# Linear attention and a Sinkhorn-routed MoE on one core: q transposed as loaded, phi read from PSUM, two scalings on GpSimd, two more units in seven products, and a new front order

## The chip, the cores and the metric

The kernel runs on one core of a Trainium2 chip. The metric is the device time of one execution in microseconds (us), lower being better: the median of the runs shown. A core has five instruction streams that matter here: TensorE (PE) multiplies matrices, VectorE (DVE) and ScalarE (ACT) work elementwise and read and write both SBUF and PSUM, GpSimd (POOL) works elementwise and issues most loads, and SyncE (SP) issues the other DMAs. Each runs its instructions in order and waits at semaphores for the others.

## The reference

Attention with B = 8, H = 8, S = 576, d = 64, then a mixture of experts on x, the attention's result as 4608 x 512:

```python
phi = lambda x: np.where(x > 0, x, np.exp(x) - 1.0) + 1.0
kv  = np.einsum('bhsd,bhse->bhde', phi(k), v)
z   = phi(k).sum(2)
x   = (phi(q) @ kv) / (phi(q) @ z[..., None] + 1e-6)   # then (B*S, H*d) = (4608, 512)
P   = np.exp(x @ w_gate - max)
for _ in range(8):
    P /= P.sum(1, keepdims=True) + 1e-9
    P /= P.sum(0, keepdims=True) + 1e-9
    P *= N / E                                      # 4608 / 8
out = sum(P[:, e:e+1] * (np.maximum(x @ w1[e], 0) @ w2[e]) for e in range(8))   # F = 1024
```

## The kernel before, in words

All matrices are multiplied in fp16. phi(x) is computed as min(max(x + 1, 1), exp(x)). x is kept transposed in SBUF, as xT (128 x 4 x 4608).

**The front: 16 head pairs.** A call of `att(b, g)` (L385) handles four heads of one batch, n = 2b + g. Its steps: load k, q, v (L406); exp(k) on ACT (L417), max(k + 1, 1) and min on DVE (L421, L425); kv and z by 36 small matmuls with tiles of 64x64 (L446), copied to kvz (L359 on ACT or L361 on DVE). For q: exp on ACT (L477), max(q + 1, 1) on DVE into tq (L480), min on DVE (L484), 36 transposes on PE from tq into the PSUM bank pair att (L469), and a copy out of PSUM to qpT (L361, L359). Then the denominator (four matmuls of 288 columns, L504), its logarithm on ACT (L516, one for each half c of the tokens), one exp of minus the logarithm for both halves (L521), the numerator (L504), and the product of both, which writes half a row pair of xT (L531). k and q of n = 0 come as f32 on SP's queue; the other q and v come as fp16 over GpSimd's queue, which converts, with k in f32 there too. Buffers for k, q and v are three deep, and a load that reuses one waits on GpSimd for the users of its buffer; everything behind it on that queue waits with it.

**The MoE.** Tokens come in nine blocks g of 512. For expert 0 layer 1 is plain (`layer1`, hq at L717: per block 8 tiles of 4 matmuls with 512 columns; relu on ACT or DVE, L722 and L724). The first block's first four tiles are computed in two halves: first the two c rows that head pair 0 gives, then those of head pair 1. Layer 2 of expert 0 is plain in some blocks (`unit_plain`, L1017: 32 matmuls of 512 columns, four copies out of PSUM) and in the others a block product in seven instead of eight parts (`unit` and `layer2`, L1133: 56 matmuls of 256 columns, four sums S of hb on DVE at L1104, and evictions in halves at L1146 to L1151). Which blocks do which is set by the constants NS = 6, NL = 4, NG = 9 in the loop at L1255 to L1265. Experts 1 to 7 run in products throughout, from about 190 us on, with their sums of weights W and T (L1059, L1073), sums S (L1104), layer-1 products (L832), and weighted evictions on DVE (L1164) and on ACT and GpSimd (L1171, L1174). SP stores x in blocks to DRAM for them (L745, L747, L780).

**The Sinkhorn** (L560 to L606) keeps the exponentials P_sb (128 x 36 x 8) and finds row and column factors Rr and cc. In each of eight iterations f_a, on DVE, does: wt = P0 * cc (L577, not in the first), sum over experts (L574 or L579), factor (L580, L581), wt = P0 * Rr written transposed (L582), and sum over tokens (L584). PE sums over partitions with a matrix of ones (L589), and f_d on DVE gives cc (L593 to L598). At the end P = P0 * cc * Rr (L604, L605). It runs from about 125 to 176 us, between the layer-1 and layer-2 units of expert 0.

**What sets the order.** Nothing is issued as the code stands. `_Plan` (L18) collects tasks with their engines, costs, dependencies and buffer slots. Its `run` places them one by one: those of the string `_FRONT` (L141) first, in exactly that order (task number and engine letter), and the rest by earliest time and priority. So each engine's instruction order is written out by hand for the front and expert 0, and follows the costs given to `add` behind that.

**The beginning.** GpSimd's load queue starts k1, v0, k2, q1, v1, q2, v2, w1 (its first 512 columns), q3, k3, w1 (the rest), v3, q4, w2 in two pieces. w1 and w2 belong to expert 0. Until data are there PE runs dummy matmuls on a zeroed tile (`f_warm`, L621, tile yw), 46 in all.

## Time and profile before

| | |
|---|---|
| median of 3 runs | 952.09 us (951.47 to 952.39) |
| the profiled execution | 951.94 us |
| its span, first to last instruction | 950.1 us |
| mean granted TensorE clock | 0.999 |
| DVE, ACT, POOL busy | 765.3, 575.8, 144.3 us |

How to read it: the span is cut into stretches, and for each the busy time of each engine is given. An instruction's row has its start, its length, engine, line, operation, output and input tiles, and in brackets the idle time of the engine just before it with what ended that. A group's row has the count, the total, the mean in ns, and the idle time before the group's members. Matmuls are pipelined: the modelled end of one lies behind the start of the next, so the distance between starts is the cost.

### The profile page before, as it was taken

Reading aid. Unit: us, or ns where it says so; the run is one execution under the profiler, and the core shown is the slowest. Engines: PE = TensorE matmul, PEld = TensorE weight load, DVE = VectorE, ACT = ScalarE, POOL = GpSimd, SP = SyncE. Lnnn points to the kernel's source line nnn. Section 1 sums busy time; section 2 is a strip of 40 time slices with the busy share of each in tenths; the row PEclk is TensorE's granted clock in tenths of the full one; section 3 lists DMA queues with packets and bytes.
Section 4 is the critical chain, followed back from the end, with each engine's and each line's share of the span. In section 5 each row is a group of like instructions: output and inputs, shape, how many; then the busy total and the mean of one; then the engine's idle time right before and its main releaser. Section 6 shows DMA issues by size and latency. Waiting matters only on the chain.

```text
span 950.1 us, 19908 instructions
## 1 busy us (share of the span) xinstructions
PE 939.9 (99%) x7816; PEld 631.7 (66%) x7816; DVE 765.3 (81%) x1479; ACT 575.8 (61%) x1025; POOL 144.3 (15%) x204
## 2 busy tenths in 40 slices
PE   9999999999999999999999999999999999999997
PEld 4444478666676666766677666766667666776665
DVE  7699899879877888788887888878887888877776
ACT  6899856666655555555555555555555555555552
POOL 5433100011111111110011111111112111111110
PEclk9999999999999999999999999999999999999999
DMA  9989793452254222652236222652226422215544
GB/s 239 265 185 235 170 230 94 122 122 78 79 126 86 75 77 78 162 122 78 79 87 119 79 78 78 152 114 70 68 67 143 111 78 78 73 45 166 167 134 134
DMA packets 82042, 112.75 MB, mean 119 GB/s; under 512 B 7324, under 2 KB 46236, under 8 KB 81948
## 3 DMA queue, kind: packets, MB, share of 16 engines
q1 hardware_dynamic: 56876, 75.59, 26.0%
q0 software_dynamic: 24320, 34.78, 19.6%
q8 instruction: 61, 1.00, 0.4%
q10 hardware_dynamic: 752, 1.11, 0.3%
q14 instruction: 33, 0.27, 0.1%
HBM read 119.69 MB, written 17.69 MB: 145 GB/s over the span
## 4 chain that ended last, share of the span: by engine, by line
PE 94%; DMA 4%; ACT 1%; DVE 1%; POOL 0%; issue 0%
PE ye L1133 35%; PE hq L832 24%; PE R L832 12%; PE Zye L832 6%; PE Zye L1133 6%; PE ye L1017 5%; PE hq L717 3%; DMA w<-in_moe_w_dram 2%; DMA vv<-in_v_dram 2%; PE kv_ps L446 1%; PE att L504 0%; PE num_ps L504 0%; PE hq L1229 0%; DMA kin<-in_k_dram 0%; PE att L469 0%; PE R L1229 0%
## 5 line engine op out<-in xcount | busy, mean ns | idle before, releaser
L1164 DVE SCALAR_TENSOR_TENSOR acc<-ye,P_sb,acc 128x256 f32<-128x256 f32 x620 | 268.4, 479 | 126.9 <-PE ye L1133 126.2
L1133 PEld LDWEIGHTS <-S 128*128 128x128 f16 x1984 | 194.0, 98 | 46.6 <-DVE S L1104 0.2
L1133 PE MATMUL ye<-T,S 128*128 128x256 f16 x1488 | 192.8, 273 | 0.0
L1174 POOL TENSOR_TENSOR acc<-acc,st 128x256 f32<-128x256 f32 x124 | 88.1, 730 | 635.2 <-ACT st L1171 624.0
L832 PEld LDWEIGHTS <-W 128*128 128x128 f16 x1248 | 122.1, 98 | 86.6
L1133 PEld LDWEIGHTS <-hb 128*128 128x128 f16 x1536 | 150.3, 98 | 42.5 <-issue 1.3
L863 ACT ACTIVATE hb<-hq 128x512 f16<-128x512 f32 x134 | 80.2, 598 | 136.6 <-PE hq L832 130.2
L832 PE MATMUL R<-xs,W 128*128 128x512 f16 (+1 forms) x560 | 150.0, 358 | 0.0
L832 PE MATMUL hq<-xs,W 128*128 128x512 f16 (+1 forms) x560 | 150.0, 358 | 0.0
L832 PE MATMUL hq<-xs,w 128*128 128x512 f16 (+1 forms) x560 | 139.7, 358 | 0.0
L832 PEld LDWEIGHTS <-w 128*128 128x128 f16 x936 | 91.5, 98 | 59.8 <-issue 0.5
L860 ACT ACTIVATE hb<-Zye 128x512 f16<-128x512 f32 x134 | 80.1, 598 | 38.5 <-PE Zye L832 38.3
L1171 ACT ACTIVATE st<-Zye,P_sb 128x256 f32<-128x256 f32 x124 | 52.5, 471 | 77.2 <-PE Zye L1133 77.0
L866 DVE CUSTOM_DVE_ANT_0 hb<-hq,sx 128x512 f16<-128x512 f32 x126 | 86.6, 687 | 15.0 <-PE hq L832 14.9
L853 ACT COPY sx<-hq 128x512 f32<-128x512 f32 x126 | 73.6, 584 | 35.3 <-PE hq L832 35.3
L849 ACT COPY Zye<-hq 128x512 f32<-128x512 f32 x134 | 77.9, 581 | 22.6 <-PE hq L832 22.4
L866 DVE CUSTOM_DVE_ANT_0 hb<-R,sx 128x512 f16<-128x512 f32 x126 | 86.5, 687 | 4.9 <-ACT sx L853 3.8
L1104 DVE TENSOR_TENSOR S<-hb 128x1024 f16<-128x1024 f16 x124 | 85.0, 686 | 5.0 <-ACT hb L863 5.0
L832 PE MATMUL Zye<-xs,w 128*128 128x512 f16 (+1 forms) x280 | 75.0, 358 | 0.0
L857 ACT COPY sx<-R 128x512 f32<-128x512 f32 x126 | 74.4, 591 | 0.0
L1133 PE MATMUL ye<-w,hb 128*128 128x256 f16 x512 | 66.3, 273 | 0.6 <-DVE acc L1164 0.5
L1133 PE MATMUL Zye<-w,hb 128*128 128x256 f16 x512 | 66.3, 273 | 0.0
(119 smaller groups left out, 940.8 us busy)
## 6 DMA issues: line engine op xcount, KB each, us to landing
xs<-xd SPq DMA_DIRECT2D x196, 256.0 KB, 3.3
w<-in_moe_w_dram POOLq DMA_DIRECT2D x18, 512.0 KB, 7.7
kin<-in_k_dram POOLq DMA_DIRECT2D x15, 576.0 KB, 7.4
out_dram<-acc SPq DMA_DIRECT2D x61, 128.0 KB, 2.4
w<-in_moe_w_dram POOLq DMA_DIRECT2D x7, 1024.0 KB, 9.8
xs<-xd SPq DMA_DIRECT2D x49, 128.0 KB, 3.2
vv<-in_v_dram POOLq DMA_DIRECT2D x16, 288.0 KB, 7.2
hb<-in_q_dram POOLq DMA_DIRECT2D x15, 288.0 KB, 6.4
```

The source lines that it names most:

```text
L832: nc.tensor.matmul(dst_[:, p, :] if parts == 2 else dst_.rearrange("p a b -> p (a b)"), lhsT=lhs(p, c), rhs=blk[i](c), start=(first and p ...
L849: nc.scalar.copy(out=Zt[1], in_=gX["tile"])
L853: nc.scalar.copy(out=gs2["tile"], in_=gX["tile"])
L857: nc.scalar.copy(out=gs5["tile"], in_=gR["tile"])
L860: nc.scalar.activation(out=dst(0, 0), in_=Zt[1], func=AF.Relu)
L863: nc.scalar.activation(out=dst(1, 0), in_=gX["tile"], func=AF.Relu)
L866: nc.vector._custom_dve(TENSOR_ADD_SAT, out=out_, in0=ps, in1=sb, s0=3.0e38, s1=0.0)
L1104: nc.vector.tensor_tensor(out=Sx[:, i], in0=a0, in1=a1, op=op)
L1133: nc.tensor.matmul(bank(g_)[:, s, :], lhsT=lhs(s, kk), rhs=rhs(kk), start=(new and s == 0 and kk == 0), stop=(kk == 3), skip_group_check=True)
L1164: nc.vector.scalar_tensor_tensor(out=dst(), in0=bank(g_)[:, s, :], scalar=P_sb[:, gg, e:e + 1], in1=dst(), op0=ALU.mult, op1=ALU.add)
L1171: nc.scalar.mul(out=gst["tile"], in_=bank(g_)[:, s, :], mul=P_sb[:, gg, e:e + 1])
L1174: nc.gpsimd.tensor_tensor(out=dst(), in0=dst(), in1=gst["tile"], op=ALU.add)
```

## The change

1. **Load order and warm-up.** GpSimd's queue begins v0, k1, q1, v1, w1 (256 columns), the identity matrix, w1 (256), q2, w1 (512), k2, q3, v2, k3, v3, w2 in two pieces; w_gate's load comes later. w1 of expert 0 is loaded in three pieces instead of two. 38 dummy matmuls instead of 46.
2. **q of n >= 1** is transposed as it was loaded; ACT takes the exp and DVE max(x + 1, 1) directly from PSUM, and the min is taken in SBUF. The copy is gone, and tq is used by n = 0 alone. For n = 1 the transposes go to two of the ye banks, and exp and max are done in halves so that both engines start at once.
3. **The exp of minus the logarithm** is done in two halves for n < 2, so that half 0 of xT doesn't wait for half 1.
4. **The Sinkhorn's two scalings** of each iteration (15 in all) run on GpSimd. wt is no longer written transposed; the sum over tokens reads it with a stride.
5. **NS = 4**: blocks 4 and 5 of expert 0 do layer 2 in seven products.
6. **`_FRONT`** is a new order of about the same length for the new tasks, and some planned costs change with it. In it expert 1's w2 is loaded before its w1. The closing of the front also waits for the last gate.

The core of the diff (the order string left out):

```diff
-    NS = 6
+    NS = 4
...
-            return load_w(moe_w1, "w1", p_w1, [[((slice(None), slice(None), slice(512 * i, 512 * i + 512)),
-                                                 512 * i, [[F, P], [P * F, NDT], [1, 512]])] for i in range(2)], e, shape=[P, NDT, F], **kw)
+            return load_w(moe_w1, "w1", p_w1, [[((slice(None), slice(None), slice(a, a + n)),
+                                                 a, [[F, P], [P * F, NDT], [1, n]])] for a, n in ((0, 256), (256, 256), (512, 512))],
+                          e, shape=[P, NDT, F], costs=(1.33, 1.33, 2.6), **kw)
...
-        ga = [S_.grp(p_att), S_.grp(p_att)]
+        ga = [S_.grp(p_ye[0]), S_.grp(p_ye[1])] if n == 1 else [S_.grp(p_att), S_.grp(p_att)]
...
-                        nc.tensor.transpose(qps()[half(r), hh, j, :], gtq["tile"][half(hh), j, r, :],
+                        nc.tensor.transpose(qin(hh)[half(r), j, :],
+                                            gtq["tile"][half(hh), j, r, :] if n == 0 else gin["q"]["tile"][half(hh), r, j, :],
                                             ident[half(hh), half(hh)])
...
+            t1 = fadd(("pe", 0.29), f_qt, deps=[tin["q"], t_id[0]], acq=ga, use=[gin["q"]], prio=pr, cfg=1)
...
+            for hs in range(2 if n == 1 else 1):
+                def f_qe(_, hs=hs):
+                    o, i = qio(geq["tile"], hs)
+                    nc.scalar.activation(out=o, in_=i, func=AF.Exp)
+
+                def f_qm(_, hs=hs):
+                    o, i = qio(gq["tile"], hs)
+                    nc.vector.tensor_scalar(out=o, in0=i, scalar1=1.0, scalar2=1.0, op0=ALU.add, op1=ALU.max)
...
+            def f_qp(_):
+                nc.vector.tensor_tensor(out=gq["tile"], in0=gq["tile"], in1=geq["tile"].rearrange("p r j d -> p r (j d)"), op=ALU.min)
...
+            def f_exh(_, c=c):
+                nc.scalar.activation(out=grd["tile"][:, c], in_=grd["tile"][:, c], func=AF.Exp, scale=-1.0)
+            if n < 2:
+                te_.append(fadd(("act", 0.62), f_exh, deps=[tl[c]], use=[grd], prio=pr))
+            elif c == 0:
+                te_ = [fadd(("act", 1.18), f_ex, deps=tl, use=[grd], prio=pr)] * 2
...
-        wc = wt.rearrange("p g e -> p (g e)").rearrange("p (e g) -> p e g", e=E)
...
+            def f_a(_):
+                nc.gpsimd.tensor_tensor(out=wt, in0=P0_sb, in1=cc[:, None, :].broadcast_to([P, NTT, E]), op=ALU.mult)
...
-                    nc.vector.tensor_tensor(out=wt, in0=P0_sb, in1=cc[:, None, :].broadcast_to([P, NTT, E]),
-                                            op=ALU.mult)
...
-                nc.vector.tensor_tensor(out=wc.rearrange("p e g -> p g e"), in0=P0_sb,
+            def f_b(_):
+                nc.gpsimd.tensor_tensor(out=wt, in0=P0_sb,
                                         in1=Rr[:, :, None].broadcast_to([P, NTT, E]), op=ALU.mult)
-                nc.vector.tensor_reduce(gs, wc, AXX.X, ALU.add)
+            def f_g(_):
+                nc.vector.tensor_reduce(gs, wt.rearrange("p g e -> p e g"), AXX.X, ALU.add)
...
-            a = add(("dve", 2.29 if it == 0 else 2.78), f_a, deps=last, prio=-200.0)
+            if it:
+                last = [add(("pool", 0.9), f_a, deps=last, prio=-200.0)]
+            a = add(("dve", 1.0), f_r, deps=last, prio=-200.0)
+            a = add(("pool", 0.9), f_b, deps=[a], prio=-200.0)
+            a = add(("dve", 0.42), f_g, deps=[a], prio=-200.0)
...
-    for i in range(46):
+    for i in range(38):
...
-    t_close = add(("none", 0.0), f_close, deps=front_ids, prio=0.0)
+    t_close = add(("none", 0.0), f_close, deps=[*front_ids, gates[15]], prio=0.0)
```

## The prediction

> **What bounds the kernel now.** I began with the page: TensorE (PE) is busy for 939.9 of 950.1 us, and the chain that ended last is 94% PE. I then asked which waits make up the rest, and in which stretches they lie.

> ```profile
> span 950.1 us, 19908 instructions
> PE 939.9 (99%) x7816; PEld 631.7 (66%) x7816; DVE 765.3 (81%) x1479; ACT 575.8 (61%) x1025; POOL 144.3 (15%) x204
> PE 94%; DMA 4%; ACT 1%; DVE 1%; POOL 0%; issue 0%
> ```

> ```profile
> PE kv_ps L446 <- DMA vv<-in_v_dram: 1.2, 2, 1.0
> PE ye L1017 <- DMA w<-in_moe_w_dram: 0.7, 1, 0.7
> PE hq L717 <- DMA w<-in_moe_w_dram: 0.6, 1, 0.6
> PE att L504 <- ACT kvz L359: 0.5, 1, 0.5
> PE ye L1133 <- DVE acc L1164: 0.5, 1, 0.5
> ```

> ```profile
> 20.00:30.00 10.00, 9.28 (x149) 4.12 (x138) 6.55 (x11) 8.32 (x13) 4.32 (x6) 1.00 1.20 235
> 30.00:40.00 10.00, 8.84 (x120) 3.95 (x118) 5.11 (x8) 7.66 (x12) 2.87 (x4) 1.00 1.16 282
> 90.00:100.00 10.00, 9.03 (x178) 4.20 (x173) 9.50 (x17) 9.41 (x15) 1.50 (x2) 1.00 0.86 205
> 110.00:180.00 70.00, 70.00 (x617) 51.34 (x606) 63.80 (x139) 43.63 (x80) 3.85 (x6) 1.00 0.65 155
> ```

> The first column pair is the stretch, the next PE's busy time. PE is full from 110 to 180 us, where the Sinkhorn runs on VectorE (DVE). It loses under 1.2 us in each of three earlier stretches, and all the waits listed there are for loads. So two things can shorten the run: PE's first **useful** MoE matmul coming earlier, or less PE work behind it. Freeing DVE time is worth nothing by itself.

> The beginning is the third view, the timeline:

> ```profile
> 1.33 8.58 PE L621 MATMUL yw<-hb 128*128 128x512 f16 x26 [1.33 <-DVE hb L611]
> ...
> 8.16 1.16 ACT L417 ACTIVATE ek<-kin 128x1152 f16<-128x1152 f32 x1 [0.92 <-DMA kin<-in_k_dram]
> ...
> 14.90 0.70 PE L446 MATMUL kv_ps<-vv,t 64*64 64x128 f16 x36 [0.24 <-DMA vv<-in_v_dram]
> ...
> 15.52 0.48 PE L469 MATMUL att<-ident,tq 64*64 64x64 f16 x36
> ...
> 15.92 0.60 PE L621 MATMUL yw<-hb 128*128 128x512 f16 x2
> 16.13 0.76 DVE L361 COPY qpT<-att 128x1152 f16<-128x1152 f16 x1
> ...
> 20.52 0.71 POOL L406 DMA_DIRECT2D kin<-in_k_dram  x1 [1.79 <-DMA w<-in_moe_w_dram]
> ...
> 20.60 1.04 PE L717 MATMUL hq<-xT,w 128*128 128x512 f16 x4
> 20.99 0.75 DVE L531 TENSOR_TENSOR xT<-num_ps,rden 128x576 f16<-128x576 f32 x1
> 21.56 0.34 PEld L504 LDWEIGHTS <-kvz 64*64 64x64 f16 x8 [0.42 <-issue]
> ...
> 22.04 2.81 PE L717 MATMUL hq<-xT,w 128*128 128x512 f16 x12
> ...
> 25.66 1.90 PE L717 MATMUL hq<-xT,w 128*128 128x512 f16 x8 [0.56 <-DMA w<-in_moe_w_dram]
> ```

> PE runs dummy matmuls (yw) until the first hq at 20.60. That one waits for the first piece of w1, eighth on GpSimd's load queue, landed just before 20.52. The next hq, at 22.04, needs the x of head pair n=1 (20.99). A 512-column matmul costs (1.90 − 1.04)/4 = 0.215 us.

> **The change part by part.**

> *1. Start: load order, q transposed as loaded, half exponentials.* The new queue is v0, k1, q1, v1, w1 (first half-size piece). Landings go by place: in the old order the first place (k1) landed by 8.16 and the fifth (v1) at about 14.9. Spaced evenly between (1.7 each), v0 is there by 8.2, k1 by 9.8, q1 by 11.5, v1 by 13.2, w1's piece by 14.9. Only 19 dummies precede, ending near 1.33 + 8.58 − 7 × 0.215 = 8.4. The durations for what follows:

> ```profile
> L531 DVE TENSOR_TENSOR xT<-num_ps,rden 128x576 f16<-128x576 f32 x27 | 20.3, 753 | 3.6 <-PE num_ps L504 3.5
> ...
> L484 DVE TENSOR_TENSOR tq<-tq,eq 128x1152 f16<-128x1152 f16 x16 | 12.1, 754 | 1.4 <-ACT eq L477 1.3
> ...
> L361 DVE COPY qpT<-att 128x1152 f16<-128x1152 f16 x14 | 10.6, 757 | 5.5 <-PE att L469 3.1 <-ACT kvz L359 2.1
> ...
> L480 DVE TENSOR_SCALAR tq<-hb 128x1152 f16<-128x1152 f16 x15 | 7.2, 477 | 0.1
> ```

> ```profile
> L516 ACT ACTIVATE rden<-att,eps_t 128x576 f32<-128x576 f32 x28 | 20.7, 738 | 4.1 <-PE att L504 3.9
> ...
> L521 ACT ACTIVATE rden<-rden 128x1152 f32<-128x1152 f32 x14 | 16.3, 1167 | 0.2
> ```

> Head pair 1: q lands at 11.5, transposes 0.4, two rounds of half-size exp and max (half of 1.16 is 0.6) 1.2, min 0.75, so phi(q) is ready near 14.0. Then den 0.3, two ln 1.5, half an exp 0.6, product 0.75, with some 0.4 of handoffs: 17.5 for the second group of hq, against 22.04, that is −4.5. Head pair 0's second xT half comes near 15.3 the same way, and the first hq follows at about 15.9 against 20.60, −4.7. I take **−4.5**; bounds −3 (v1 only where the old fifth place landed, 14.9) and −5.2.

> Not all of this is gain, since one kv and one set of transposes that stood ahead of the first hq now stand behind it: 0.62 (14.90 to 15.52) plus 0.40 (15.52 to 15.92), and four switches between tile shapes at about 0.1 each (the four hq from 20.60 are issued by 21.46, the next weights load at 21.56): **+1.4**.

> Per later n, DVE replaces 0.477 + 0.754 + 0.757 by max(x+1, 1) from PSUM and 0.754. No row shows that operation from PSUM. Its bounds are 0.757 (the f16 PSUM copy, same shape) and 1.54 (the f32 relu from PSUM below, 686 ns for 512 columns, scaled to 1152). I take 0.757 as the nearest, which saves DVE 0.48 for each of 15. PE isn't short of DVE there (9.03 and 9.28 above, lost to loads), so: nothing.

> ```profile
> L724 DVE TENSOR_SCALAR hb<-hq 128x512 f16<-128x512 f32 x11 | 7.5, 686 | 0.4 <-PE hq L717 0.4
> ```

> *2. Loads after the start.* hq work begins 4.5 earlier, but w2 of expert 0 doesn't: of the loads ahead of it only one (q4, 288 KB, about 1.5 us) has gone behind. Before, PE lost 0.56 and 0.68 to w (rows above), with mode switches and the wait inside the next unit some 2.35 us up to 40 us. From the first hq to the first ye lay 31.1 − 20.6 = 10.5 us, about 0.8 of it wait. Now that work would run out at about 15.9 + 9.7 + 1.4 = 27, while w2 lands near 31.1 − 1.5 = 29.6, or one place sooner, 28.2. Two to three us of wait then stand where 2.35 stood: I take 3.0, **+0.7** (bounds −1 and +2).

> ```profile
> L1017 PE MATMUL ye<-w,hb x224: 376/379/390, 31.1 to 186.7; 128*128 128x512 f16 x112
> ```

> The last v of the front cost PE 1.0 (in the 90 to 100 stretch). Its issue follows buffers that PE frees, so it moves up with the work, though not by all of it: **+0.4** (0 to +2).

> *3. Two more layer-2 units in seven products.* Each replaces 32 matmuls of 512 columns by 56 of 256 columns. The medians of the two widths differ by 379 − 273 = 106 ns for 256 columns, so the price is proportional to the width: 32 × 0.215 − 56 × 0.108 = 0.83 each, twice: **−1.6** (rounding −1.66 down for the extra weight loads). DVE gets 8 sums at 0.686 and smaller evictions; part 4 frees more.

> ```profile
> L1133 PE MATMUL ye<-T,S 128*128 128x256 f16 x1488 | 192.8, 273 | 0.0
> ```

> *4. Sinkhorn scalings on GpSimd.* DVE loses 8 × 0.675 + 7 × 0.453 = 8.6 us. The strided reduce of gs may now cost up to what the strided write cost, 675 instead of 453; I take 0.453, the upper end being +1.8 of DVE time.

> ```profile
> L582 DVE TENSOR_TENSOR wt<-P_sb,Rr 128x288 f32<-128x288 f32 x8 | 5.4, 675 | 0.3
> L584 DVE TENSOR_REDUCE gs<-wt 128x8 f32<-128x288 f32 x8 | 3.6, 453 | 0.3
> L577 DVE TENSOR_TENSOR wt<-P_sb,cc 128x288 f32<-128x288 f32 x7 | 3.2, 453 | 0.1
> ```

> GpSimd's own price isn't in the trace; the nearest row is a 256-column product sum:

> ```profile
> L1174 POOL TENSOR_TENSOR acc<-acc,st x124: 713/726/989, 194.9 to 937.6; 128x256 f32<-128x256 f32 x124
> ```

> That gives 726 × 288/256 = 0.82 us, bounds 0.453 (DVE's) and 0.82 × 675/453 = 1.22 (if a broadcast operand costs GpSimd what the stride cost DVE). The waiting instruction is DVE's reduce of wt: behind it on DVE stand the relus, sums and evictions that free PE's PSUM. The written order plans 0.9 per scaling and puts two or three DVE operations (0.4 to 0.7 each) in between, so 0.82 is covered. [...]

> But the covering operations disturb it. GpSimd took 800 and 953 ns beside DVE work where 726 is its median, and DVE's 0.69 product took 0.94 beside a GpSimd sum:

> ```profile
> 224.41 0.80 POOL L1174 TENSOR_TENSOR acc<-acc,st 128x256 f32<-128x256 f32 x1 [4.46 <-ACT st L1171]
> 231.38 0.95 POOL L1174 TENSOR_TENSOR acc<-acc,st 128x256 f32<-128x256 f32 x1 [6.17 <-ACT st L1171]
> ```

> ```profile
> 250.00 0.94 DVE L1073 TENSOR_TENSOR T<-w 128x1024 f16<-128x1024 f16 x1
> ```

> Fifteen scalings at up to 0.25 each bound this at 0 to 3.75. DVE has slack there (63.80 busy of 70), so I take 0.3 of that: **+1.1**. [...]

> **Sum:** −4.5 + 1.4 + 0.7 + 0.4 − 1.6 + 1.1 = −2.5. The profiled execution took 951.94 (span 950.1 and 1.84 around it), 0.15 below the median of 952.09. So 951.94 − 2.5 = **949.4**.

> **The rivals.**

> *A, slower: GpSimd's scaling sets the Sinkhorn's pace.* [...] It is slower than before by over 0.2% from a scaling of about 1.13 us (4.6/15 = 0.31 above 0.82). For it: 953 and 989 occur. Against: 726 is the median. 0.15.

> *B, no change: the loads take the start back.* PE reaches the later loads 2 to 2.5 us earlier and waits for them by as much, most of all for the last v: 949.4 + 2.1 = 951.5. For it: all the waits of the front are for loads. Against: 9.03 in its worst stretch shows only 1 us lost. 0.20.

> [...] 0.17.

> *D, the q part doesn't do what it says:* max from PSUM at 1.54 adds 0.3 a head pair to DVE instead of saving 0.48, and the front, where DVE is 9.50 of 10 busy, stretches by 15 × 0.3 = 4.5 at most: up to 953.9. 0.05.

> **How the numbers follow.** The forecast keeps 0.43, with 948 to 951 as its own range. 0.2% of 952.09 is 1.9, about what a measurement of this kernel can tell from no change, so faster means below 950.2 and slower above 954.0. Faster: 0.31 of the forecast, all of C, 0.04 of B: 0.52. Slower: 0.12 of A and 0.02 of D: 0.14. The rest, 0.34, is the same. The range 946.8 to 954.3 reaches from C to A's near edge; most of A and C's far tail are left out.

> **What would show it.** The first hq at 15.5 to 16.3, the next group near 17.5 (step 1). A wait of PE for w of 2 to 3 us between 24 and 30 (step 2). L1017's count down by 64 and 256-column matmuls up by 112. The max from PSUM near 0.76. GpSimd's scalings near 0.82, some at 1.0, and PE in the Sinkhorn losing about 1 us (step 4). The prediction is wrong if scalings take over 1.1 us, if PE idles there for several us, or if PE's waits for v or k after 70 us grow beyond 2 us.

## The result, and the profile after

The changed kernel is **slower**: 956.6 us (median of five runs, 955.74 to 960.11) against 951.87 for the kernel before on the same chip, a ratio of 1.0056 with a 95% interval of 1.0036 to 1.0077. The forecast was 949.4, with a range from 946.8 to 954.3. The profiled execution is the longest of the five (960.11, 3.5 above the median) and has the lowest mean granted clock (0.996, the others 0.998 and 0.999), so a single loss read from it can be larger than in the others. On a second chip (`a0_again`, below) the same kernel has 959.0, ratio 1.0069 (1.0051 to 1.0087).

Lines have moved by up to 64: the transposes of q are L484 (were L469), the first layer of expert 0 L781 (L717), its plain second layer L1081 (L1017), products L896 and L1197 (L832 and L1133), GpSimd's weighted sum L1238 (L1174), weight loads L337 (L335), loads of x from DRAM L873 (L809). Two names in the texts above were exchanged: the first k in the old queue belongs to head pair 2, the third place holds k1, and in the new order head pair 3 is loaded ahead of 2. The places in the queue, on which the argument rests, are as given.

The page of the changed kernel:

```profile
span 958.3 us, 19980 instructions
PE 940.5 (98%) x7856; PEld 636.7 (66%) x7856; DVE 772.2 (81%) x1477; ACT 569.8 (59%) x1015; POOL 156.5 (16%) x220
PE 80%; DVE 4%; DMA 1%; issue 0%; POOL 0%; DVEq 0%; POOLq 0%
```

PE is as busy as before (940.5 against 939.9) but its span is 8.2 longer: the loss is waiting. DVE, GpSimd and DMA have taken places in the chain. PE's waits, with the sum in us, the number of times and the longest:

```profile
PE att L484 <- DMA hb<-in_q_dram: 3.2, 4, 1.3
PE R L896 <- DMA xs<-xd: 2.0, 1, 2.0
PE Zye L896 <- DMA xs<-xd: 1.5, 1, 1.5
...
PE kv_ps L454 <- DMA vv<-in_v_dram: 1.1, 1, 1.1
...
PE R L649 <- DVE gs L644: 0.9, 2, 0.4
```

The first three rows are new against before. PE's transposes wait for q, and the experts' first products (R, Zye) for x. The stretches (PE's busy time stands behind the length, then PEld, DVE, ACT, POOL, the granted clock, the share of DMA and GB/s):

```profile
26.00:28.00 2.00, 0.98 (x33) 0.59 (x36) 1.90 (x3) 1.58 (x3) 0.90 (x2) 1.00 1.24 206
28.00:30.00 2.00, 1.47 (x38) 0.64 (x27) 1.80 (x4) 1.80 (x3) 0.26 (x1) 0.72 1.24 209
30.00:32.00 2.00, 2.00 (x13) 0.45 (x12) 1.01 (x3) 0.36 (x1) 0.47 (x1) 0.50 1.11 347
50.00:60.00 10.00, 9.08 (x181) 4.85 (x170) 8.26 (x14) 8.06 (x10) 4.40 (x6) 1.00 1.11 244
70.00:80.00 10.00, 8.63 (x187) 4.45 (x186) 8.94 (x17) 8.86 (x13) 2.88 (x4) 1.00 1.07 198
90.00:100.00 10.00, 8.55 (x155) 4.08 (x154) 8.25 (x13) 7.85 (x11) 1.00 (x2) 1.00 1.12 246
120.00:180.00 60.00, 58.94 (x557) 51.02 (x556) 56.48 (x122) 35.16 (x66) 13.48 (x17) 1.00 0.55 132
206.00:208.00 2.00, 0.03 (x2) 0.01 (x1) 1.78 (x4) 0.60 (x2) 0.00 (x0) 1.00 1.16 285
```

There are four places of loss. Around 30 us the clock falls to a half after a stretch in which PE was half idle. Between 50 and 100 us PE misses 0.92, 1.37 and 1.45 in three stretches, with three of the four waits for q (0.82, 1.30 and 0.35). In the Sinkhorn it misses 1.06 of 60, where before it missed nothing. At 206 us it stands still. The timeline of the changed kernel shows the start and the third place (start, length, instruction; in brackets the idle time before it):

```profile
16.14 1.04 PE L781 MATMUL hq<-xT,w 128*128 128x512 f16 x4
...
17.78 1.04 PE L781 MATMUL hq<-xT,w 128*128 128x512 f16 x4
...
208.00 0.61 PE L896 MATMUL R<-xs,W 128*128 128x512 f16 x2 [1.97 <-DMA xs<-xd]
210.08 1.01 PE L896 MATMUL Zye<-xs,w 128*128 128x512 f16 x2 [1.48 <-DMA xs<-xd]
```

The start is as forecast: hq at 16.14 and 17.78. What holds x up at 208 is on the two load queues. First GpSimd's in the changed kernel, then SP's:

```profile
198.07 0.73 POOL L1238 TENSOR_TENSOR acc<-acc,st 128x256 f32<-128x256 f32 x1 [24.92 <-ACT st L1235]
198.74 2.43 POOL L337 DMA_DIRECT2D w<-in_moe_w_dram  x3
```

```profile
200.43 5.52 SPq L873 DMA_DIRECT2D xs<-xd  x7
```

And both in the kernel before:

```profile
166.55 1.41 POOL L335 DMA_DIRECT2D w<-in_moe_w_dram  x2 [50.02 <-PE hq L832]
...
200.01 0.73 POOL L1174 TENSOR_TENSOR acc<-acc,st 128x256 f32<-128x256 f32 x1 [4.43 <-ACT st L1171]
200.68 0.92 POOL L335 DMA_DIRECT2D w<-in_moe_w_dram  x1
```

```profile
197.23 5.52 SPq L809 DMA_DIRECT2D xs<-xd  x7
```

Before, two of expert 2's three weight loads went out at 166.55, and the third, of 1 MB, at 200.68, 3.5 us **behind** the start of the loads of x. In the changed order all three (2 MB) stand behind GpSimd's first weighted sum and start at 198.74, 1.7 us **ahead** of x. The loads issued from 196 to 216 us in the changed kernel (count, KB each, median us from issue to landing):

```profile
xs<-xd SPq DMA_DIRECT2D x7, 256.0 KB, 11.7
w<-in_moe_w_dram POOLq DMA_DIRECT2D x1, 1024.0 KB, 12.7
```

Over the whole execution an x load takes 3.4.

For one ledger, an estimate, I compared the two traces where the same PE work is left: the time of each stretch, corrected by the PE work already done. By that the start gains 4.5 to 4.8; the stretch from 22 to 33 us loses about 1, and 1.7 more in the execution in which the clock falls; 50 to 100 us loses 2.5 to 3; the Sinkhorn 2.2 to 2.4 (the idle 1.06, and matmuls lengthened by waits inside a group); and the collision at 204 to 215 some 5. The ranges sum to +5.9 to +8.6, and the two profiled executions of the changed kernel (this one and that of `a0_again`) lie 8.2 and 6.4 above the kernel before's. What each place is worth is for the experiments.

### The profile page after: what moved, and what is told of

The parts are those of the page before. It is cut to its first block, busy times and chain, and to the rows that moved or that the text cites. A ratio compares the mean times of both kernels' runs of the same rounds, so it can differ in the third digit from the quotient of the medians.

```text
span 958.3 us, 19980 instructions
## 1 busy us (share of the span) xinstructions
PE 940.5 (98%) x7856; PEld 636.7 (66%) x7856; DVE 772.2 (81%) x1477; ACT 569.8 (59%) x1015; POOL 156.5 (16%) x220
## 4 chain that ended last, share of the span: by engine, by line
PE 80%; DVE 4%; DMA 1%; issue 0%; POOL 0%; DVEq 0%; POOLq 0%
PE ye L1197 34%; PE hq L896 22%; PE R L896 11%; PE Zye L1197 6%; PE Zye L896 6%; DVE hb L930 1%; DMA xs<-xd 1%; DVE xT L1168 1%; PE ye L1081 1%; PE hq L1293 0%; DVE gs L644 0%; PE R L1293 0%; DVE acc L1215 0%; DVE ut L635 0%; DVE acc L1228 0%
## 5 line engine op out<-in xcount | busy, mean ns | idle before, releaser
L1197 PEld LDWEIGHTS <-S 128*128 128x128 f16 x1984 | 194.2, 98 | 46.9 <-DVE S L1168 0.2
L1197 PE MATMUL ye<-T,S 128*128 128x256 f16 x1488 | 193.1, 273 | 0.0
L1238 POOL TENSOR_TENSOR acc<-acc,st 128x256 f32<-128x256 f32 x124 | 88.3, 731 | 636.5 <-ACT st L1235 620.9
L1197 PEld LDWEIGHTS <-hb 128*128 128x128 f16 x1584 | 155.3, 98 | 43.7 <-issue 1.7
L896 PEld LDWEIGHTS <-W 128*128 128x128 f16 x1248 | 122.1, 98 | 88.4 <-DMA xs<-xd 2.5
L896 PE MATMUL R<-xs,W 128*128 128x512 f16 (+1 forms) x560 | 150.1, 358 | 2.0 <-DMA xs<-xd 2.0
L896 PE MATMUL hq<-xs,W 128*128 128x512 f16 (+1 forms) x560 | 150.0, 358 | 0.0
L896 PE MATMUL hq<-xs,w 128*128 128x512 f16 (+1 forms) x560 | 139.8, 358 | 0.1
L896 PEld LDWEIGHTS <-w 128*128 128x128 f16 x936 | 91.7, 98 | 61.3 <-issue 2.4
L896 PE MATMUL Zye<-xs,w 128*128 128x512 f16 (+1 forms) x280 | 75.4, 359 | 1.5 <-DMA xs<-xd 1.5
L1197 PE MATMUL ye<-w,hb 128*128 128x256 f16 x528 | 69.3, 275 | 0.5 <-DVE acc L1228 0.5
L1197 PE MATMUL Zye<-w,hb 128*128 128x256 f16 x528 | 68.4, 273 | 0.0
```

Source lines behind the costliest of these rows:

```text
L896: nc.tensor.matmul(dst_[:, p, :] if parts == 2 else dst_.rearrange("p a b -> p (a b)"), lhsT=lhs(p, c), rhs=blk[i](c), start=(first and p ...
L1197: nc.tensor.matmul(bank(g_)[:, s, :], lhsT=lhs(s, kk), rhs=rhs(kk), start=(new and s == 0 and kk == 0), stop=(kk == 3), skip_group_check=True)
L1238: nc.gpsimd.tensor_tensor(out=dst(), in0=dst(), in1=gst["tile"], op=ALU.add)
```

## The experiments

All variants have the complete order of all 5064 tasks written out, so that an edit moves only what it names. The ratios are to the kernel before on the same chip.

**a0_again: the changed kernel once more.** No edit.

> The changed kernel once more, instruction for instruction. The profiled execution of it lost 5.2 us between 205 and 215 us (PE waited 1.97 and 1.48 us for the x blocks of expert 1 and its granted clock stood at 0.50 from 210 to 212), and its clock stood at 0.50 from 29 to 32 us. If these belong to the program's order, this run shows both again and its time is near 956.6. If the stretch at 205 is an accident of one execution, it is missing here, the span is near 954, and the clock over the span is 0.998 or 0.999 instead of 0.996.

Measured: 959.0 us (957.53 to 960.59), 1.0069 (1.0051 to 1.0087). Its profiled execution has the waits for x again (2.0 and 1.2), but not the half clock near 30 us:

```profile
28.00:30.00 2.00, 1.46 (x16) 0.53 (x12) 1.82 (x4) 1.80 (x2) 0.55 (x1) 1.00 1.22 211
30.00:32.00 2.00, 1.99 (x18) 0.79 (x19) 1.22 (x2) 1.47 (x2) 0.21 (x2) 1.00 1.10 338
```

PE idles as much as in the first profile (1.46 against 1.47 of 2) and the clock stays at 1.00. So the slowdown is reproduced, and the half clock near 30 us isn't needed for it. Behind the waits for x this execution has half clock too, from 207.7 to 211.1.

**e1_w1_early: two of the three weight loads as early as before.** The 1 MB load stays where it is.

```diff
-665a 1139g ... 1197d 1519g 1520m ... 1201d 1521g 1522m
+665a 1519g 1521g 1139g ... 1197d 1520m ... 1201d 1522m
```

> One edit of order: expert 2's two loads of w1 are issued ahead of GpSimd's first weighted sum (and so before expert 1's second group of x loads), as in the kernel before, where they were issued at 166.55; in the changed kernel they stand behind that sum and were issued at 199.68 and 200.36, together with 1 MB of w2, on top of seven x loads from 200.43 on. Theory (the weights crowd out the x loads): no wait of PE for xs, and 1 to 5 us off the changed kernel's time on the same chip. Rival (the x loads are late for another reason, such as their own issue): PE's wait for xs stays and the time is the changed kernel's within 0.5 us.

Measured: 957.88 (957.66 to 959.21), 1.0056 (1.0039 to 1.0072). The two loads now start from 171.75 on, but PE waits as before:

```profile
PE R L896 <- DMA xs<-xd: 2.0, 1, 2.0
...
PE Zye L896 <- DMA xs<-xd: 1.4, 1, 1.4
```

The theory in this form fell: it isn't the number of bytes ahead of x. With the single 1 MB load, issued at 197.81, 1.7 us before x (199.48), the waits are as long.

**e2_dve: the scalings back on VectorE**, with the transposed write of before, in the changed order.

```diff
-                nc.gpsimd.tensor_tensor(out=wt, in0=P0_sb,
+                nc.vector.tensor_tensor(out=wc.rearrange("p e g -> p g e"), in0=P0_sb,
...
-                nc.vector.tensor_reduce(gs, wt.rearrange("p g e -> p e g"), AXX.X, ALU.add)
+                nc.vector.tensor_reduce(gs, wc, AXX.X, ALU.add)
```

> Undoes part 4 alone: the 15 scalings of the Sinkhorn stand on VectorE at the place where GpSimd had them, wt is written transposed again and the sum over tokens reads it in order. Theory (moving them to GpSimd costs more than it frees: the strided sum takes 666 instead of 453 ns, eight times 0.21, operations beside GpSimd's take 0.06 to 0.15 longer, and VectorE stands waiting for wt): the stretch from 120 to 180 us gets about 2.4 us shorter. Rival (VectorE is full there, 9.5 to 9.8 of 10, because of the two more units in products, and GpSimd relieved it): VectorE gets 8.6 us of scalings back for some 4 us saved, and the time gets 3 to 5 us longer.

Measured: 963.73 (963.21 to 964.18), 1.0118 (1.0103 to 1.0133), 4.7 us above `a0_again`. The Sinkhorn's stretch:

```profile
120.00:180.00 60.00, 54.83 (x518) 47.13 (x516) 56.27 (x131) 31.54 (x59) 0.00 (x0) 1.00 0.51 124
```

PE now misses 5.17 instead of 1.06, with DVE at 56.27 of 60. So GpSimd's part is not a loss: in this order it is worth about 5 us. PE's waits in that stretch, 2.2, 1.6 and 1.1, are all for VectorE, which has no slack for the scalings there. (In the kernel before, whose order and work in that stretch are different, VectorE carries the scalings and PE misses nothing.)

**e3_contig: GpSimd writes transposed, VectorE sums contiguously.** The diff is that of e2 with `nc.gpsimd` kept.

> The scalings stay on GpSimd, but f_b writes wt transposed there, so that VectorE's sum over tokens reads in order. Theory (the strided sum is on the path: VectorE is full): the sum goes from 666 to about 450 ns, 1.7 us of VectorE's time, and the time falls by 1 to 1.7 us if GpSimd's transposed write costs no more than its plain one (778 ns); if that write takes 1.2 us instead, the time rises by 2 us or more. Rival (the chain through GpSimd sets the pace and not VectorE's work): no change within 0.5 us.

Measured: 955.85 (955.28 to 959.43), 1.0040 (1.0023 to 1.0057), 3 us below `a0_again`. The groups of the changed kernel first (total us, mean ns, idle before them), then those of this one:

```profile
L640 POOL TENSOR_TENSOR wt<-P_sb,Rr 128x288 f32<-128x288 f32 x8 | 6.2, 778 | 18.0 <-DVE Rr L637 12.4 <-ACT acc L363 5.6
L628 POOL TENSOR_TENSOR wt<-P_sb,cc 128x288 f32<-128x288 f32 x7 | 5.8, 834 | 22.1 <-DVE cc L658 22.1
L644 DVE TENSOR_REDUCE gs<-wt 128x8 f32<-128x288 f32 x8 | 5.3, 666 | 0.6 <-POOL wt L640 0.6
```

```profile
L640 POOL TENSOR_TENSOR wt<-P_sb,Rr 128x288 f32<-128x288 f32 x8 | 6.4, 805 | 18.0 <-DVE Rr L637 12.4 <-ACT acc L363 5.6
L644 DVE TENSOR_REDUCE gs<-wt 128x8 f32<-128x288 f32 x8 | 3.6, 446 | 0.7 <-POOL wt L640 0.7
```

```profile
120.00:180.00 60.00, 59.73 (x566) 51.92 (x563) 55.59 (x124) 36.32 (x68) 13.69 (x17) 1.00 0.58 139
```

The stride costs GpSimd 27 ns as a write and VectorE 220 ns as a read. Eight times 220 is 1.8 us of VectorE time, and PE in the Sinkhorn goes from 58.94 to 59.73 busy. The time fell by more than the expected 1 to 1.7, but the difference of the ratios, 0.0029, has an interval of some 0.0025 either way. What is left there is small.

**e4_weights_after: expert 2's 1 MB load behind x.** To the edit of e1 comes:

```diff
-1196d 1524g 1525m 1199a ... 1207g 1213d
+1196d 1199a ... 1207g 1524g 1525m 1213d
```

> One edit of order: expert 2's w1 is issued ahead of GpSimd's first weighted sum, and its w2 (1 MB) behind the fourth, so that nothing large stands ahead of the second group of seven x loads. With w1 alone moved, PE's waits for xs stayed (2.0 and 1.4), with w2 issued 1.7 us ahead of the first x load; in the kernel before w2 came after six of the seven. Theory (any large weight load issued just ahead of the x loads makes them late): no wait of PE for xs, no clock of 0.50 around 208, and some 5 us off the profiled execution of the changed kernel (958.3), so about 953 to 954. Rival (the x loads are late by their own issue, 3 us later than before): the waits stay, and the time is 957 to 959.

Measured: 953.61 (952.51 to 956.84), 1.0029 (1.0018 to 1.0039). The two queues and the stretch:

```profile
213.50 0.91 POOL L337 DMA_DIRECT2D w<-in_moe_w_dram  x1
```

```profile
201.46 5.52 SPq L873 DMA_DIRECT2D xs<-xd  x7
```

```profile
206.00:208.00 2.00, 2.00 (x13) 1.02 (x12) 1.80 (x4) 1.29 (x3) 0.00 (x0) 1.00 0.92 277
```

PE is full where it stood still, although the x loads are issued later than in the changed kernel (201.46 against 200.43), so their own issue isn't the cause. Against the changed kernel's 1.0056 and 1.0069 the ratio falls by 0.0027 to 0.0040, that is by 2.6 to 3.8 us: the collision is shown, and by the medians it is worth about 3 us, less than the 5 of the profiled executions. These medians contain half clock as well: of e4's ten runs four have a mean clock of 0.999 or 1.000 and took 952.5 to 953.3, the other six 0.996 to 0.998 and 953.5 to 956.8; its profiled execution, at 0.996, has none around 208, but 6.8 us of it from 28.7 on.

**e5_keep_busy: dummy matmuls in PE's waits between 23 and 29 us**, to hold the clock up.

```diff
+        def keep(m, y="ye1"):
+            t = yps.tile([P, 512], FP32, tag=y, name="yk")
+            for _ in range(m):
+                nc.tensor.matmul(t, lhsT=w_t[0][0]["tile"][:, 0, 0:P], rhs=w_t[0][0]["tile"][:, 0, 0:512], start=True, stop=True)
...
+            if n == 2:
+                keep(3)
...
+                if n == 3 and c == 1:
+                    keep(4)
```

(and 2 and 3 more at n = 2 and 3, twelve in all)

> Twelve dummy matmuls of 512 columns (2.6 us of PE time at full clock) stand in PE's order ahead of the four waits between 23 and 29 us; nothing else is changed. Theory (the waits cost their length, about 2.4 us, and where PE idles so much in a few us its clock is granted at 0.50 afterwards for 3 to 4 us, which costs another 1.5 to 2): the granted clock stays at 1.00 between 26 and 36 us, and the time is 1 to 2 us below that of the executions that had the drop, with no gain over one without it. Rival (the clock drops for another reason): the clock is 0.50 there all the same, and the time rises by the dummies' share that does not fit into the waits.

Measured: 958.42 (956.75 to 959.93), 1.0074 (1.0059 to 1.0090).

```profile
28.00:30.00 2.00, 2.00 (x50) 0.94 (x49) 1.25 (x3) 1.69 (x2) 0.55 (x1) 1.00 1.26 219
30.00:32.00 2.00, 2.00 (x20) 0.71 (x16) 1.98 (x3) 1.32 (x2) 0.18 (x1) 1.00 1.10 339
...
208.00:210.00 2.00, 1.42 (x5) 0.69 (x5) 0.00 (x0) 0.00 (x0) 0.00 (x0) 0.50 1.11 268
```

The clock stays up at 30 us, but the expected 1 to 2 us didn't come. In the profiled execution half clock lasts 6.8 us at 208 where the changed kernel has 3.4 there and 3.4 near 30, so this execution has as much of it as the changed kernel's. This run alone doesn't tell whether the dummies cost what they save. `e8_three` takes the question up.

**e6_q_order: q loaded earlier for the head pairs that wait.** In GpSimd's queue the q loads of head pairs 7, 10 and 13 change places with those of later head pairs that stood ahead of them: 9 ahead of 7, 11 ahead of 10, and 14 and 15 ahead of 13.

```diff
-192d 307g 308m ... 236n 251g 252m ... 297a 361g 362m ... 322d 334g 335m
+192d 251g 252m ... 236n 307g 308m ... 297a 334g 335m ... 322d 361g 362m
...
-371p 444g 445m ... 375d 474g 475m ... 397n 417g 418m
+371p 417g 418m ... 375d 444g 445m ... 397n 474g 475m
```

> Only the order in which GpSimd issues q loads is changed: q of head pairs 7, 10 and 13 change places with q of 9, 11 and of 14 and 15, so that each lands before PE wants to transpose it. Theory (q transposed as loaded puts the landing of q directly on PE's queue; PE waited 0.8, 1.3 and 0.35 us for these three): these waits are gone and the time falls by 1.5 to 2.5 us. Rival (the front is held by the length of the chain from q to xT or by the other loads, and the wait moves to the next instruction): PE waits as long for something else between 55 and 100 us, and the time changes by less than 0.7 us.

Measured: 955.2 (953.0 to 957.18), 1.0036 (1.0016 to 1.0056). The wait for q that remains, and the three stretches:

```profile
PE att L484 <- DMA hb<-in_q_dram: 0.5, 1, 0.5
```

```profile
50.00:60.00 10.00, 9.90 (x173) 5.00 (x163) 8.83 (x14) 8.84 (x12) 4.33 (x6) 1.00 1.11 251
70.00:80.00 10.00, 9.93 (x215) 5.08 (x204) 9.87 (x18) 9.63 (x15) 4.63 (x7) 1.00 1.07 197
90.00:100.00 10.00, 9.56 (x161) 4.86 (x160) 9.08 (x16) 8.82 (x14) 0.83 (x2) 1.00 0.84 209
```

PE regains 0.82, 1.30 and 1.01, together 3.1 us, and the ratio falls by 0.0020 to 0.0033 (1.9 to 3.1 us). So the waits for q are a loss of their own and pass through to the end. (The interval overlaps that of the changed kernel's first run; e7 and e8 bear it out.) No byte fewer is loaded; only the order in the queue was wrong. The wait that remains is the one at 23 us, which this edit doesn't touch.

**e7_all_four: the edits of e3, e4, e5 and e6 together.**

> The four repairs together: contiguous sum (scalings still on GpSimd, f_b writing transposed), weights of expert 2 around the x loads, q loads in order of use, and the twelve dummy matmuls. If each of the causes is worth what it seemed alone (1.6, 5.0, 2.0 and up to 2.0 us off an execution at 958.3) and they add up, the time is 948 to 950, that is 2 to 4 us below the kernel before. If the losses hide one another, it stays above 952.

Measured: 949.62 (948.54 to 949.95), 0.9980 (0.9970 to 0.9989), against 951.18. This beats both kernels, and is what was expected if the losses add up.

**e8_three: e7 without the dummies.**

> The version with the four repairs, less its twelve dummy matmuls: PE idles again between 23 and 29 us. Theory (the idling itself is no loss that dummies could repair, but the clock that is granted after it is): where the clock falls to 0.50 behind it, the time is 1.5 to 2.5 us above the version with dummies, near 951.5; where it does not fall, the time is within 0.5 us of it. So the median lies 0.5 to 2.5 above, and the runs scatter by 2 us instead of 1.4. Rival (the dummies are worth nothing): same time within 0.4 us and the same scatter.

Measured: 949.17 (948.22 to 949.56), 0.9967 (0.9954 to 0.9980), against 951.92.

```profile
28.00:30.00 2.00, 1.47 (x28) 0.54 (x16) 1.80 (x4) 1.94 (x3) 0.40 (x1) 1.00 1.25 219
30.00:32.00 2.00, 1.99 (x19) 0.79 (x19) 1.37 (x3) 1.32 (x2) 0.33 (x1) 1.00 1.08 328
120.00:180.00 60.00, 59.61 (x513) 49.45 (x512) 54.75 (x120) 36.48 (x68) 14.87 (x19) 1.00 0.63 162
```

The expectation that it would be 0.5 to 2.5 above e7 failed: PE idles as long as in the changed kernel, and the clock stays at 1.00 without a dummy. All five runs have a mean clock of 0.999 or 1.000, as have the nineteen of e7 and e9.

**e9_four_again: e7 beside e8 on the same chip.**

> The version with the four repairs once more, beside the one without dummies on the same chip. Its ten runs lay between 948.54 and 949.95; expected 949.0 to 950.0 again, and a granted clock of 1.00 in every stretch up to 900 us.

Measured: 949.73 (948.76 to 950.55), 0.9977 (0.9967 to 0.9987). With and without dummies can't be told apart here, so the three edits of e8 carry the whole gain. Counted one by one from 957.9 for the changed kernel (952 x 1.0056 to 1.0069 is 957.3 to 958.6), the mean of its two ratios less those of e4, e3 and e6 (0.0033, 0.0022 and 0.0026, each times 952) gives 3.2, 2.1 and 2.5: 957.9 − 7.8 = 950.1. By its ratio e8 is at 952 x 0.9967 = 948.9, and e7 and e9 at 949.8 to 950.1. The three losses are separate and add up, within the intervals. e8 has no half clock in its profiled execution where each single repair has 6.8 us or more; the share of that isn't separated.

## Why the prediction was wrong, point by point

Three steps failed: step 2 counted the loads of w2 and v but not those of q; the sum had no term for expert 2's weights and the x loads; and the Sinkhorn's term was too small. By the repairs they cost some 2.5, 3.2 and 2.1 us; the sum had 1.1 for the last and nothing for the other two.

**Start (−4.5, moved work +1.4, products −1.6): right.** Forecast 15.9 and 17.5, measured 16.14 and 17.78 against 20.60 and 22.04. The ledger's −4.5 to −4.8 for the start, which counts the moved work and the products as well, stands beside a forecast of −4.7 for the three terms. For the products e8 agrees: its PE is busy for 3.5 us less than before (936.4 against 939.9), of which eight dummies fewer at 0.215 are 1.7, and 1.8 are left.

**Max from PSUM (0.757): right within about 6%.** Thirteen of these operations, from the groups of the changed kernel:

```profile
L536 DVE TENSOR_SCALAR qpT<-att 128x1152 f16<-128x1152 f16 x13 | 10.4, 803 | 3.1 <-ACT eq L532 2.8 <-PE num_ps L553 0.2
```

The median of all fourteen is 758, and the two from 106 us on took 1.36 us. Rival D (1.54) is out.

**Step 2, loads after the start (+0.7 and +0.4): wrong.** The step looked for waits at w2 and at the last v, and rival B for more of those. In size the first of them came, by luck: PE misses about 2.3 us between 20 and 30 us where 2 to 3 were forecast, and the first matmul of layer 2 starts at 29.51 (31.1 before). But none of it is a wait for w. It is this, in the changed kernel's timeline:

```profile
23.03 0.48 PE L484 MATMUL att<-ident,hb 64*64 64x64 f16 x36 [0.72 <-DMA hb<-in_q_dram]
...
27.16 0.32 PE L553 MATMUL att<-qpT,kvz 64*64 64x288 f16 x4 [0.84 <-ACT rden L565]
...
28.88 0.46 PE L553 MATMUL num_ps<-qpT,kvz 64*64 64x288 f16 x4 [0.53 <-DVE kvz L365]
```

Only the first is a wait for a load. The others, with 0.18 more for VectorE, are 1.55 of the 2.27. The prediction had read all waits of the front as waits for loads; in its own list ACT's kvz (0.5) and VectorE's acc (0.5) aren't. Nor did the last v get dearer (1.1, before 1.0).

What the step overlooked is the order of the q loads in part 6 of the change. In the old order q of the head pairs 1 to 12 is loaded in the order of use. The new one loads 8 and 9 ahead of 7, and 11 ahead of 10, although PE still transposes 7 and 10 first (14 and 15 stand ahead of 13 in both). Before, q of 7 was issued at 34.62 and first read at 55.35, and q of 10 at 57.68 and 74.70, which is 20.7 and 17.0 us later. For head pair 7 the changed kernel has:

```profile
50.16 0.80 POOL L411 DMA_DIRECT2D hb<-in_q_dram  x1 [0.96 <-PE att L484]
```

```profile
56.90 0.48 PE L484 MATMUL att<-ident,hb 64*64 64x64 f16 x36 [0.82 <-DMA hb<-in_q_dram]
```

PE was ready for it at 56.08, 5.9 us behind the issue, and for that of 10 at 77.18, 4.8 us behind 72.40. A q load took 6.7 us there (median from 40 to 100 us). Part 2 takes away some slack as well: before, the max and the min (0.477 and 0.754, 1.2 us at least) stood between q and PE's transposes, and now PE itself meets the landing, in order, with everything behind it. How much of the waits that adds is not shown; margins of 17 us and more leave room for it. Cost of the order of q by e6: 1.9 to 3.1.

**Not in the sum at all: expert 2's weights.** The prediction treated everything behind the front as unchanged in its order, so these loads had no term. But the order string covers the first 2234 tasks (2192 before), and with them GpSimd's queue from 166 to 214 us. A 1 MB load went from 3.5 us behind the x loads to 1.7 us ahead. Cost by e4: 2.6 to 3.8. This is the largest miss by the middle of the ranges, and it would be enough to take the forecast out of "faster".

**Sinkhorn (+1.1): the direction right, the size too small.** GpSimd's scalings were put at 0.82 and took 778 and 834 ns. The operations beside them got longer as feared, as VectorE's 1024-column sums show (here in the changed kernel from 105 to 190 us; in e2, with no scaling on GpSimd, the same sums have a mean of 684; why they get longer, no run shows):

```profile
L1168 DVE TENSOR_TENSOR xT<-hb 128x1024 f16<-128x1024 f16 x8 | 6.0, 747 | 0.0
```

But the strided sum was taken at 453 (upper end 675) and took 666, so the upper end (+1.8 of DVE time) was due. The prediction also held that freeing DVE time is worth nothing by itself and that DVE has slack there; e2 contradicts that for this order, where the scalings put back on VectorE cost 4.7. Rival A (scalings of 1.13 or more) did not come about: the time it stands for, above 954.0, was reached for other reasons. Cost by e3: 1.5 to 2.8 of the ledger's 2.2 to 2.4.

**The clock.** The forecast didn't reckon with it. In the traces a stretch of half clock lasts 3.41 us or about twice that (below). The one near 30 us cost 1.4: the changed kernel's two profiled executions, one with and one without it, stand at 28.88 and 28.58 at the numerator where it begins, and at 36.16 and 34.44 at the transposes of head pair 4. The mean clock of a run counts it: 0.999 or 1.000 in the profiled executions without any ahead of the span's last us, 0.998 with 3.4 us of it, 0.996 with 6.8, 0.995 with some 10 in e3. By that the medians have a share of it too. Of the changed kernel's five runs the two at 0.999 took 955.74 and 956.02, the two at 0.998 956.60 and 957.11, and the one at 0.996 960.11.

That e8 lies where the forecast did (949.17 against 949.4) doesn't confirm the forecast's terms: its waits between 20 and 30 us have other causes than the ones added up, and its order is not the one that was forecast.

**What stays open.** No run shows how the gain of e8 splits between the three repairs and the half clock that it doesn't have, nor what the 1 MB load costs when it alone is moved. The wait for x is dearer in the profiled executions (some 5) than between the medians of e4 and the changed kernel (some 3); half clock behind it is up to 1.7 of the 5 (an estimate, half of its 3.41 us), and not every run has it, but no run separates the rest. The two added product units and the new order of the front were not tried by themselves.

## What to carry to other kernels

When an order is rewritten, check that every load still stands in the order of use: a margin of 17 to 21 us became one of 5 to 6 by loading 9 ahead of 7 and 11 ahead of 10. Compare every large load, too, with the neighbours it gets on all queues, also a hundred microseconds behind the place that was meant: one 1 MB load 1.7 us ahead instead of 3.5 behind cost 3 us. And put a stride on the engine that has time, after measuring both sides: the same transposition cost 27 ns as a write of GpSimd and 220 as a read of VectorE.

## What the runs showed of the hardware

In the changed kernel's trace the two stretches of half clock last 3.41 us each and start at 28.87 and 209.78, which is 53 times 3.413 us apart. By the mean clock of the windows a stretch lasts some 3.4 us in `a0_again`, e1 and e6 too, and some 6.8 in e4 and e5. When the changed kernel's execution is cut into intervals of 3.413 us, counted both ways from 28.87, PE was busy for 1.87 and 0.61 us in the two just before the clock fell, and for 2.11 or more in all others from 1.6 to 953.8 us; the clock was back at 1.00 after one interval of half clock each, with 3.40 and 3.11 busy. In the interval from 25.46 to 28.87, the one with 1.87, none of the waits was longer than 0.84. In `a0_again` half clock begins near 207.7; intervals counted back from there cut the same waits in two, with some 2.7 and 2.6 busy (an estimate from its timeline), and the clock stayed at 1.00. Whether the place of the cut decides, no run tried. The clock was 0.50 also in the last 1.0 us of the kernel before and of the changed one, with PE already done.

GpSimd's scaling, with two inputs of which one is broadcast, took 805 ns with a strided write (e3) against 778 without (the changed kernel), while VectorE's sum took 666 ns with a strided read (the changed kernel) against 446 (e3). VectorE's 1024-column sums have a mean of 747 ns beside the scalings, and 684 in e2, which has none on GpSimd. Of the eight in the changed kernel the two that began during a scaling (at 148.21 and 163.38) took 1.02 and 0.92 us, the other six 0.63 to 0.69.
